# Masks of the scores in a fixed order, the first query load on a second queue, and a planner with other lengths

## The chip, the cores and the metric

The kernel runs on one NeuronCore of a Trainium2 chip. The metric is the device time of one execution in microseconds. The median of three runs of the kernel before is 693.08 us (692.32 to 693.16).

The engines are named as in the profile: PE (matrix multiply; PEld is its weight load), DVE (vector), ACT (scalar), POOL (GpSimd) and SP (the queue that issues nearly all transfers).

## The reference

Windowed attention with four sink keys, over 4 batches, 8 heads, 768 positions and head size 64, is followed by a feed-forward layer over the 3072 tokens (512 to 2048 to 512).

```python
scores = (q @ k.T) / sqrt(64)
keep = (pos_k < n_sink) | ((pos_q - pos_k >= 0) & (pos_q - pos_k < window))   # n_sink 4, window 128
scores = where(keep, scores, -1e9)
a = exp(scores - max); a = a / (sum(a) + 1e-9)
x = (a @ v) with the heads side by side                                     # 3072 x 512
h = x @ w_in                                                                # 512 x 2048
g = where(h >= 1, h, where(h <= -1, 0, (h + 1)**2 / 4))
out = g @ w_out
```

The weights arrive as 64-bit floats and `n_sink` and `window` as 64-bit integers; the kernel takes them apart on the chip.

## The kernel before

**Tiling.** A unit is one batch, one head and 384 query rows, that is three tiles of 128. The first 32 units (query rows 0 to 383 of each head) come first and the other 32 after them. For the first 16 units (batches 0 and 1) two heads make a pair: `pair_scores` (L630 to L673) multiplies queries by keys (L648, PE), adds the mask and takes the row peak (L658, DVE) and does the exponential with its sum (L667, ACT). `pair_sums` (L678, L680, DVE) inverts the sums; `early_transp` transposes the probabilities on PE (L690, L692) and ACT copies them out (L699, L696, L697); `pair_r` and `pair_av` multiply by the inverse sums and the values (L733, L713 on PE, L738 on ACT, L720 on DVE). Four such pairs are one batch, and their result is the tile `xn`. Units of the later batches go through `scores`, `transp` and `av` (L444, L449, L459 to L471, L525, L587).

**Feed-forward.** `split` (L851 ACT, L852 DVE) writes `xn` as a high and a low part `x`, in four pieces of 128 columns. `stage1` (L811 PE) and `stage2` (L834 PE) run over 16 column groups of the hidden layer, each with three matmuls in place of one. Between them stand L818, L819 and L822 on ACT and L820 and L823 on DVE. From the second batch on, this work and the attention of a later batch alternate on PE.

**Weights.** `block(n)` brings one of 16 blocks of 1 MB (L359) and turns it from 64-bit words into a high and a low part: L361, L363, L365 on DVE, L367 on ACT, L368 on DVE. Even blocks belong to `w_in`, odd ones to `w_out`. The first `stage1` needs block 0 and all four pieces of `x` of the first batch, which needs pairs 0 to 3.

**Masks.** Four tiles that hold 0 or a large negative number are made at the start from positions (written by POOL) and from the two parameters `n_f` and `w_f`: `m0` for the first query tile, `m1n` for the second tile of a pair, `m2` for the third, and `m1` for later units.

**What sets the order.** The steps of attention, feed-forward and weights are recorded with `op(engine, length, ...)`. The class `Plan` gives every step a due time, reckoned backwards from PE with the lengths in the code, and writes each engine's queue in the order of a list schedule; a load on SP becomes eligible 3000 or 8000 ns ahead of its due time (L136) and counts as landed 1900 ns after its bytes (L182). After that each engine runs its queue strictly in the order written. The code ahead of the recorded steps (masks, constants) is ordered by the framework. The call that switches that off, `manual_schedule`, stands behind the masks (L398).

Of the kernel before, what the change touches and what calls it, by code (L numbers as in the profile page):

```python
# [197 lines left out]
def attn_ffn(ctx, tc, qk, qkp, vx, vs, par, w_in, w_out, out):  # L198
# [46 lines left out]
    peak = const.tile([P, B * H * NT // CT, CT], F32, name="peak")  # L245

    scr = xpool.tile([P, 1032], F32, name="x")  # L250
    mi = scr[:, 0:260].bitcast(I32)
    rel, kpos, skp, ge0 = scr[:, 260:520], scr[:, 520:648], scr[:, 648:776], scr[:, 776:904]
    ki = scr[:, 904:1032].bitcast(I32)
    nc.gpsimd.iota(mi[:, 0:P], pattern=[[-1, P]], base=P, channel_multiplier=1)
    nc.gpsimd.iota(mi[:, P:KB], pattern=[[-1, NSINK]], base=0, channel_multiplier=0)
    nc.gpsimd.iota(mi[:, KB:260], pattern=[[-1, P]], base=0, channel_multiplier=1)
    nc.vector.tensor_copy(rel, mi)
    nc.gpsimd.iota(ki, pattern=[[1, P]], base=0, channel_multiplier=0)
    nc.vector.tensor_copy(kpos, ki)
    nc.vector.tensor_scalar(skp, kpos, n_f, None, op0=ALU.is_lt)  # L260
    m2 = const.tile([P, 260], F32, name="m2")
    m1 = const.tile([P, 260], F32, name="m1")
    m1n = const.tile([P, 260], F32, name="m1n")
    m0 = const.tile([P, P], F32, name="m0")
# [2 lines left out]
    nc.vector.tensor_tensor(m2[:, KB:260], m2[:, KB:260], ge0, op=ALU.mult)
    nc.vector.tensor_copy(m2[:, P:KB], skp[:, 0:NSINK])
    nc.vector.tensor_copy(m1, m2)
    nc.vector.tensor_copy(m1n, m2)  # L270
    nc.vector.tensor_tensor(m1n[:, 0:P], m2[:, 0:P], skp, op=ALU.max)
    behind = nc.gpsimd.memset(m1n[:, P:KB], 0.0).ins
    nc.vector.tensor_tensor(m0, m2[:, KB:260], skp, op=ALU.max)
    nc.vector.tensor_scalar(skp, kpos, n_f, None, op0=ALU.is_ge)
    nc.vector.tensor_tensor(m1[:, 0:P], m1[:, 0:P], skp, op=ALU.mult)
# [4 lines left out]
    with tc.issue_after(behind):  # L280
        R = 2 * CT * NSINK
        tsel2 = const.tile([120, 2, CT], F32, name="tsel2")
        tsel = const.tile([120, CT], F32, name="tsel")
        nc.gpsimd.memset(tsel2, 0.0)
        for r0 in (0, 32, 64, 96):
            t = tsel2[r0:r0 + R]
            nc.gpsimd.memset(t, 1.0)
            nc.gpsimd.affine_select(out=t, in_=t, pattern=[[-CT * NSINK, 2], [-NSINK, CT]], base=0, channel_multiplier=1,
                                    compare_op=ALU.is_ge, fill=0.0)
            nc.gpsimd.affine_select(out=t, in_=t, pattern=[[CT * NSINK, 2], [NSINK, CT]], base=NSINK - 1,  # L290
                                    channel_multiplier=-1, compare_op=ALU.is_ge, fill=0.0)
        nc.gpsimd.tensor_tensor(tsel, tsel2[:, 0], tsel2[:, 1], op=ALU.add)
        sk1 = const.tile([120, P], F32R, name="sk1")
        nc.gpsimd.memset(sk1.bitcast(F32), 0.0)
        sks = [const.tile([P, 2, CT * NSINK], F32, name=f"sinks{i}") for i in range(2)]
        for t in sks:
            nc.gpsimd.memset(t, 0.0)

        sp = [const.tile([P, CT * P], F32R, name=f"sp{i}") for i in range(2)]
        vsx = [const.tile([P, 2, D], F32R, name=f"vsx{i}") for i in range(2)]  # L300
        for t in sp + vsx:
            nc.gpsimd.memset(t.bitcast(F32), 0.0)
# [775 lines left out]
```

## Time and profile before

| what | value |
|---|---|
| median of three runs | 693.08 us |
| the profiled execution, as timed | 692.49 us |
| its span in the trace | 690.4 us |
| PE busy | 674.4 us, 98% of the span |
| DVE, ACT, POOL busy | 509.6, 487.2, 240.5 us |
| chain that ended last, by engine | PE 90%, DVE 5%, ACT 2%, DMA 1% |

The timed value is 2.1 us above the span and lies inside the spread of the three runs. PE is the engine that is nearly always busy, so the time is read from where PE stands still and from what comes due at those places. A busy share says little about DVE, ACT and the transfers here; their waits in the first 40 us say more. The times in the rows are microseconds from the start of the span.

### The profile page before, as it was taken

How to read it: one execution, taken by the hardware profiler on the slowest of the kernel's cores; microseconds unless marked ns; L12 is line 12 of the kernel's file. 1: busy time of each engine (PE TensorE's matmuls, PEld its weight loads, DVE VectorE, ACT ScalarE, POOL GpSimd, SP SyncE). 2: the span in 40 equal slices, each digit the busy share in tenths (PEclk: the TensorE clock that was granted, in tenths of full speed). 3: DMA queues.
4: the chain of work that ended last, by engine and by line, in shares of the span. 5: the costliest groups of instructions: out<-in, count | busy, mean ns of one | idle time of the engine just before them, and what ended most of it. 6: DMA issues, size and time to landing. Idle time of an engine off the chain costs nothing.

```text
span 690.4 us, 11991 instructions
## 1 busy us (share of the span) xinstructions
PE 674.4 (98%) x3889; PEld 603.1 (87%) x3889; DVE 509.6 (74%) x1421; ACT 487.2 (71%) x1241; POOL 240.5 (35%) x421
## 2 busy tenths in 40 slices
PE   6999999999999999999999999999999999999995
PEld 4677788889999999999999999999999999999994
DVE  7998999887767777787887877887778777733221
ACT  6977776776768788786778777797777866544332
POOL 3000023444434444453553554444463454300000
PEclk9999999999999999999999999999999999999999
DMA  7756353232222433434434443344433231000001
GB/s 230 272 218 217 113 203 105 61 91 62 54 85 91 152 109 103 138 92 142 134 105 121 134 140 94 126 123 134 127 104 104 66 98 33 1 31 16 1 1 51
DMA packets 41086, 73.94 MB, mean 107 GB/s; under 512 B 4344, under 2 KB 25656, under 8 KB 41016
## 3 DMA queue, kind: packets, MB, share of 16 engines
q1 hardware_dynamic: 41016, 73.09, 33.7%
q8 instruction: 33, 0.54, 0.3%
q14 instruction: 37, 0.30, 0.1%
HBM read 66.78 MB, written 6.29 MB: 106 GB/s over the span
## 4 chain that ended last, share of the span: by engine, by line
PE 90%; DVE 5%; ACT 2%; DMA 1%; issue 1%; SPq 0%; POOL 0%; DVEq 0%; ACTq 0%
PE h_ps L811 37%; PE o_ps L834 37%; PE ps_a L587 5%; PE ps_a L444 5%; PE ps_a L525 2%; DMA w<-w_in 1%; PE ps_a L713 1%; PE ps_a L690 1%; PE ps_a L648 1%; DVE x L852 1%; PE ps_a L733 1%; PE ps_a L602 1%; DVE p L471 0%; DMA q_h<-qkp 0%; DVE gl L823 0%
## 5 line engine op out<-in xcount | busy, mean ns | idle before, releaser
L811 PE MATMUL h_ps<-x,wi 128*128 128x384 f32 x1536 | 311.6, 340 | 0.6 <-DVE x L852 0.6
L811 PEld LDWEIGHTS h_ps<-x,wi 128*128 128x128 f32 x1536 | 262.3, 188 | 10.8 <-issue 1.9
L834 PE MATMUL o_ps<-w,gh 128*128 128x512 f32 x768 | 243.4, 398 | 0.0
L834 PE MATMUL o_ps<-w,gl 128*128 128x512 f32 x384 | 151.0, 393 | 0.0
L834 PEld LDWEIGHTS o_ps<-w,gh 128*128 128x128 f32 x768 | 134.1, 188 | 15.7 <-issue 1.4
L426 POOL TENSOR_TENSOR q_l<-r,q_h 128x384 fp32r<-128x384 f32 x48 | 50.1, 1043 | 206.9 <-ACT q_h L425 202.8
L820 DVE SCALAR_TENSOR_TENSOR g<-g,h_ps 128x384 f32<-128x384 f32 x128 | 70.3, 549 | 61.4 <-ACT g L819 60.7
L818 ACT ACTIVATE g<-h_ps,half 128x384 f32<-128x384 f32 x128 | 74.0, 578 | 56.9 <-PE h_ps L811 55.7
L823 DVE TENSOR_TENSOR gl<-g,gh 128x384 fp32r<-128x384 f32 x128 | 78.9, 616 | 31.1 <-ACT gh L822 30.1
L452 ACT ACTIVATE p<-p,peak 128x260 f32<-128x260 f32 (+1 forms) x144 | 71.7, 498 | 40.9 <-DVE peak L449 40.3
L822 ACT CAST gh<-g 128x384 fp32r<-128x384 f32 x128 | 65.3, 510 | 43.8 <-DVE g L820 42.8
L834 PEld LDWEIGHTS o_ps<-w,gl 128*128 128x128 f32 x384 | 72.0, 188 | 16.9
L449 DVE CUSTOM_DVE_ANT_0 p<-ps_a,m 128x260 f32<-128x260 f32 (+1 forms) x144 | 57.6, 408 | 23.6 <-PE ps_a L444 23.2
L819 ACT ACTIVATE g<-g 128x384 f32<-128x384 f32 x128 | 67.3, 526 | 3.5
L471 DVE CUSTOM_DVE_ANT_0 p<-p,stat 128x128 f32<-128x128 f32 x128 | 62.4, 512 | 2.4
L546 POOL TENSOR_SCALAR_AFFINE_SELECT pt<-pt 128x384 fp32r<-128x384 f32 (+1 forms) x96 | 50.8, 535 | 21.8 <-ACT pt L534 12.8
L551 POOL TENSOR_SCALAR_AFFINE_SELECT pt<-pt 128x384 fp32r<-128x384 f32 (+1 forms) x96 | 50.7, 548 | 0.1
L498 POOL TENSOR_TENSOR v_s<-r,v_s 128x256 fp32r<-128x256 f32 (+1 forms) x48 | 37.2, 774 | 37.4 <-ACT v_s L497 31.7
L587 PEld LDWEIGHTS ps_a<-pt,v_s 128*128 128x128 f32 x304 | 42.5, 188 | 2.3
L587 PE MATMUL ps_a<-pt,v_s 128*128 128x256 f32 (+1 forms) x304 | 41.8, 275 | 0.0
L444 PE MATMUL ps_a<-k_s,q_l 128*128 128x260 f32 (+1 forms) x144 | 40.4, 281 | 0.0
L444 PE MATMUL ps_a<-k_s,q_h 128*128 128x260 f32 (+1 forms) x144 | 39.7, 276 | 0.2 <-DVE xn L606 0.2
(158 smaller groups left out, 856.4 us busy)
## 6 DMA issues: line engine op xcount, KB each, us to landing
r<-qk SPq DMA_DIRECT2D x48, 192.0 KB, 2.4
k_r<-qk SPq DMA_DIRECT2D x32, 262.0 KB, 2.8
w<-w_in SPq DMA_DIRECT2D x8, 1024.0 KB, 7.3
again<-w_in SPq DMA_DIRECT2D x16, 512.0 KB, 4.2
again<-w_out SPq DMA_DIRECT2D x16, 512.0 KB, 3.7
w<-w_out SPq DMA_DIRECT2D x6, 1024.0 KB, 7.5
out<-o SPq DMA_DIRECT2D x23, 256.0 KB, 2.9
r<-vx SPq DMA_DIRECT2D x32, 128.0 KB, 2.0
```

Of the source, the lines that this page charges most:

```text
L444: nc.tensor.matmul(ps()[:, lo:260], lhsT=q()[:, i * P:(i + 1) * P], rhs=k_s()[:, c0:c0 + 260 - lo], start=(j == 0), stop=(j == len(qs) - 1))
L449: op(DVE, 215 if lo else 350, lambda: nc.vector.tensor_tensor_reduce(out=p()[:, i, lo:260], in0=ps()[:, lo:260], in1=m, scale=-0.125, scal ...
L452: op(ACT, 400 if lo else 500, lambda: nc.scalar.activation(p()[:, i, lo:260], p()[:, i, lo:260], AF.Exp, bias=peak[:, n, i:i + 1], scale=-1.0,
L471: nc.vector.tensor_tensor_reduce(out=own, in0=own, in1=p()[:, k, 0:P], scale=r, scalar=0.0, op0=ALU.add, op1=ALU.add, accum_out=stat()[:, ...
L587: nc.tensor.matmul(z, lhsT=w, rhs=y, start=(n == 0), stop=(n == len(mms) - 1))
L811: nc.tensor.matmul(h_ps()[:, :T], lhsT=w_i[j][:, w, ct * P:(ct + 1) * P], rhs=x()[:, y, ct], start=(ct == 0 and n == 0), stop=(ct == NCT - ...
L818: op(ACT, 490, lambda: nc.scalar.activation(g(), h_ps()[:, :T], AF.Relu, bias=half, scale=0.5), r=[h_ps], w=[g])
L819: op(ACT, 440, lambda: nc.scalar.activation(g(), g(), AF.Square), w=[g])
L820: op(DVE, 470, lambda: nc.vector.scalar_tensor_tensor(g(), g(), 1.0, h_ps()[:, :T], op0=ALU.min, op1=ALU.max), r=[h_ps], w=[g])
L822: op(ACT, 420, lambda: nc.scalar.copy(gh(), g()), r=[g], w=[gh])
L823: op(DVE, 500, lambda: nc.vector.tensor_tensor(gl(), g(), gh().bitcast(F32), op=ALU.subtract), r=[g, gh], w=[gl])
L834: nc.tensor.matmul(ps(), lhsT=gg()[:, tt * P:(tt + 1) * P], rhs=w_o[j][:, w], start=(j == 0 and n == 0), stop=(j == NJ - 1 and n == 2))
```

## The change

Masks: `manual_schedule` now begins ahead of the masks, so that they stand in the queues as they are written. They are made in fewer steps (for example, `nw` by three small operations in place of five; a comparison and the multiplication by the large negative number in one operation). `m2` and `m1` are finished by three copies on ACT and two operations on POOL. Two clears move from DVE to POOL.

Loads: the parameters and the queries of pair 0 are issued by ACT in place of SP. The query load is not a recorded step: it is written where `pair_load(0)` is called, behind `later_masks()`.

Planner: a weight block whose due time is under 25000 ns becomes eligible 6500 ns ahead in place of 3000 ns, and a block counts as landed 3400 ns after its bytes in place of 1900. The lengths of three kinds of PE steps rise.

```diff
-  max(o.ready, o.due - (3000 if o.due < 25000 else 8000)) if o.eng == SP else o.ready
+  max(o.ready, o.due - (8000 if o.due > 25000 else 6500 if o.bytes == 1 << 20 else 3000)) if o.eng == SP else o.ready
...
-                end = link + 1900
+                end = link + (3400 if o.bytes == 1 << 20 else 1900)
...
+    region.enter_context(tc.manual_schedule())
-    nc.sync.dma_start(par_i, par.rearrange("p (v w) -> p v w", w=2))
+    nc.scalar.dma_start(par_i, par.rearrange("p (v w) -> p v w", w=2))
...
-    nc.vector.tensor_scalar(m2, rel, w_f, None, op0=ALU.is_lt)
...
-    for m in (m0, m1, m1n, m2):
-        nc.vector.tensor_scalar(m, m, -1.0, -NEG, op0=ALU.add, op1=ALU.mult)
+    nc.vector.scalar_tensor_tensor(nw, low, 0.0, high, op0=ALU.is_lt, op1=ALU.add)
+    nc.vector.scalar_tensor_tensor(nw, nw, 2.0 ** 32, low, op0=ALU.mult, op1=ALU.add)
+    nc.vector.tensor_scalar(nw, nw, 0.0, float(S), op0=ALU.max, op1=ALU.min)
+    nc.vector.tensor_scalar(skn, kpos, n_f, NEG, op0=ALU.is_ge, op1=ALU.mult)
+    nc.vector.scalar_tensor_tensor(ahead, rel[:, KB:260], w_f, ahead, op0=ALU.is_ge, op1=ALU.max)
+    nc.vector.tensor_tensor(m0, ahead, skn, op=ALU.mult)
+    nc.vector.scalar_tensor_tensor(m1n[:, 0:P], rel[:, 0:P], w_f, skn, op0=ALU.is_ge, op1=ALU.mult)
+    nc.vector.tensor_scalar(m1n[:, KB:260], ahead, NEG, None, op0=ALU.mult)
+    def later_masks():
+        nc.vector.tensor_scalar(m2[:, 0:P], rel[:, 0:P], w_f, NEG, op0=ALU.is_ge, op1=ALU.mult)
+        nc.scalar.copy(m2[:, P:KB], skn[:, 0:NSINK])
+        nc.scalar.copy(m2[:, KB:260], m1n[:, KB:260])
+        nc.scalar.copy(m1[:, P:260], m2[:, P:260])
+        nc.gpsimd.tensor_scalar(skp, kpos, n_f, NEG, op0=ALU.is_lt, op1=ALU.mult)
+        nc.gpsimd.tensor_tensor(m1[:, 0:P], m2[:, 0:P], skp, op=ALU.add)
+    later_masks()
...
-        op(SP, 420, lambda: nc.sync.dma_start(q_h().bitcast(F32), qkp[b, h // 2, :, 0:T]), w=[q_h], size=P * T * 4)
+        if m:
+            op(SP, 420, lambda: nc.sync.dma_start(q_h().bitcast(F32), qkp[b, h // 2, :, 0:T]), w=[q_h], size=P * T * 4)
+        else:
+            nc.scalar.dma_start(q_h().bitcast(F32), qkp[b, h // 2, :, 0:T])
...
-        op(PE, 340 if lo else 430, mm, r=[q_s, k_s], w=banks)
+        op(PE, (400 if lo else 530) if m < H // 2 else 610 if lo else 840, mm, r=[q_s, k_s], w=banks)
...
-        op(PE, 1400, mm, r=[(pt0[a], "t", k) for a in range(2) for k in range(2)]
+        op(PE, 1450 if m < H // 2 else 1640, mm, r=[(pt0[a], "t", k) for a in range(2) for k in range(2)]
...
-        op(PE, 700, mm, r=[(stat, "r")], w=[ps])
+        op(PE, 750 if m < H // 2 else 1010, mm, r=[(stat, "r")], w=[ps])
...
-        nc.vector.memset(t, 0.0)
+        nc.gpsimd.memset(t, 0.0)
```

The line numbers of the changed kernel are its own: L659 there is L658 before, L679 is L678, L721 is L720, L853 is L852, L457 is L459. L361 to L368 are the same in both. In brackets stands which engine's work an instruction waits for.

**ACT, start of the program.** Before, behind the table load the queue goes straight to the exponentials of pair 0:

```order
L667 ACT_TABLE_LOAD
L667 ACTIVATE p_204,stat_212<-p_204,peak_97 128x128 [waits DVE_49]
L667 ACTIVATE p_210,stat_212<-p_210,peak_97 128x128 [waits DVE_49]
L667 ACTIVATE p_204,stat_212<-p_204,peak_97 128x260 [waits DVE_49] x2
L667 ACTIVATE p_210,stat_212<-p_210,peak_97 128x260
```

and in the changed kernel, from the parameters' load to the first exponential (`x_88` holds `skn`, `q_h_178` the queries of pair 0):

```order
L227 DMA par_i_81<-par 128x4
L272 ACT_TABLE_LOAD
L272 COPY m2_84<-x_88 128x4 [waits DVE_49]
L273 COPY m2_84<-m1n_86 128x128 [waits DVE_49]
L274 COPY m1_85<-m2_84 128x132 [waits Activation_49]
L619 DMA q_h_178<-qkp 128x384
L668 ACTIVATE p_197,stat_205<-p_197,peak_83 128x128 [waits DVE_49]
```

The load of pair 0's queries, which was the third one on SP, stands on ACT behind three copies of masks, two of which wait for DVE.

**DVE, behind the scores of pair 2.** Before (`w_246` is block 0, `stat_285` the sums of pair 1, `xn_163` the output of pair 0):

```order
L361 TENSOR_SCALAR ends_181<-w_246 128x1024
L720 TENSOR_TENSOR xn_163<-ps_a_308,xn_163 128x384
L678 TENSOR_SCALAR stat_285<-stat_285 128x2x3
L680 RECIPROCAL stat_285<-stat_285 128x2x3
L363 TENSOR_SCALAR ends_181<-w_246 128x1024
L365 SCALAR_TENSOR_TENSOR w_246<-w_246,ends_181 128x1024
L658 ISA pt_239,peak_97<-o_ps_355,m0_109 128x128
```

and now (`w_236` is block 0, `stat_275` the sums of pair 1, `ps_a_303` the output of pair 0, `pt_234` and `pt_224` hold pair 3):

```order
L679 TENSOR_SCALAR stat_275<-stat_275 128x2x3
L681 RECIPROCAL stat_275<-stat_275 128x2x3
L721 TENSOR_TENSOR xn_159<-ps_a_303,xn_159 128x384
L361 TENSOR_SCALAR ends_175<-w_236 128x1024
L659 ISA pt_234,peak_83<-o_ps_349,m0_87 128x128
L659 ISA peak_83 128x1
L659 ISA pt_234,peak_83<-o_ps_355,m1n_86 128x260
L659 ISA peak_83 128x1
L363 TENSOR_SCALAR ends_175<-w_236 128x1024
```

The first step of block 0 moved from ahead of the sums and output of pairs 1 and 0 to behind them, and the other two steps moved in among and behind the scores of pair 3.

**DVE, from the sums of pair 2 on.** Before (`stat_328` are these sums, `w_288` is block 1, `w_341` block 2):

```order
L678 TENSOR_SCALAR stat_328<-stat_328 128x2x3
L680 RECIPROCAL stat_328<-stat_328 128x2x3
L363 TENSOR_SCALAR ends_181<-w_288 128x1024
L365 SCALAR_TENSOR_TENSOR w_288<-w_288,ends_181 128x1024
L361 TENSOR_SCALAR ends_181<-w_341 128x1024
L720 TENSOR_TENSOR xn_163<-ps_a_443,xn_163 128x384
L678 TENSOR_SCALAR stat_399<-stat_399 128x2x3
L680 RECIPROCAL stat_399<-stat_399 128x2x3
L368 TENSOR_TENSOR wi0_155<-w_246,wi0_155 128x2x512
L852 TENSOR_TENSOR x_481<-xn_163,x_481 128x384
```

and now (`stat_317` are these sums, `w_236` and `w_277` blocks 0 and 1):

```order
L679 TENSOR_SCALAR stat_317<-stat_317 128x2x3
L681 RECIPROCAL stat_317<-stat_317 128x2x3
L659 ISA pt_234,peak_83<-h_ps_361,m2_84 128x260
L659 ISA peak_83 128x1
L659 ISA pt_224,peak_83<-h_ps_357,m1n_86 128x260
L659 ISA peak_83 128x1
L659 ISA pt_224,peak_83<-o_ps_351,m0_87 128x128
L659 ISA peak_83 128x1
L365 SCALAR_TENSOR_TENSOR w_236<-w_236,ends_175 128x1024
L721 TENSOR_TENSOR xn_159<-ps_a_377,xn_159 128x384
L361 TENSOR_SCALAR ends_175<-w_277 128x1024
```

Three score steps of pair 3, the third step of block 0, the output of pair 1 and the first step of block 1, which stood ahead of these sums, stand behind them now. Up to the fourth `x` piece the last step of block 1 has come in as well; before, it stood behind that piece.

**DVE, first unit of the third batch** (`spare` is the last weight block, `stat` the sums of that unit). Before:

```order
L361 TENSOR_SCALAR ends_181<-spare_182 128x1024
L459 TENSOR_SCALAR stat_1307<-stat_1307 128x3
L462 RECIPROCAL stat_1307<-stat_1307 128x3
L471 ISA p_1299,stat_1307<-p_1299,stat_1307 128x128
L471 ISA stat_1307 128x1
L471 ISA p_1299,stat_1307<-p_1299,stat_1307 128x128
L471 ISA stat_1307 128x1
L469 TENSOR_SCALAR p_1299<-p_1299,stat_1307 128x128
L363 TENSOR_SCALAR ends_181<-spare_182 128x1024
L365 SCALAR_TENSOR_TENSOR ends_181<-spare_182,ends_181 128x1024
```

and now:

```order
L361 TENSOR_SCALAR ends_175<-spare_176 128x1024
L447 ISA p_1298,peak_83<-ps_a_1316,m2_84 128x260
L447 ISA peak_83 128x1
L447 ISA p_1341,peak_83<-ps_a_1320,m0_87 128x128
L447 ISA peak_83 128x1
L363 TENSOR_SCALAR ends_175<-spare_176 128x1024
L365 SCALAR_TENSOR_TENSOR ends_175<-spare_176,ends_175 128x1024
L457 TENSOR_SCALAR stat_1303<-stat_1303 128x3
L460 RECIPROCAL stat_1303<-stat_1303 128x3
L469 ISA p_1298,stat_1303<-p_1298,stat_1303 128x128
L469 ISA stat_1303 128x1
```

The second and third step of the last block moved ahead of the unit's sums. On PE the unit's transposes (L525) moved behind two groups of three L834 matmuls.

## Rows read from the trace of the kernel before

**Rows 1.** Whom PE waited for in the whole span: us in total, times, longest us.
```profile
PE o_ps L648 <- DMA q_h<-qkp: 4.6, 1, 4.6
PE ps_a L690 <- DVE stat L678: 1.6, 1, 1.6
PE ps_a L525 <- DVE p L469: 0.9, 1, 0.9
PE h_ps L811 <- DVE x L852: 0.6, 1, 0.6
```

**Rows 2.** Stretches: length; busy PE, PEld, DVE, ACT, POOL; granted clock; DMA share, GB/s.
```profile
34.00:110.00 76.00, 75.85 (x467) 60.56 (x468) 70.17 (x135) 54.45 (x131) 5.46 (x4) 1.00 0.54 187
150.00:680.00 530.00, 530.00 (x2969) 486.14 (x2968) 375.36 (x1080) 373.99 (x937) 208.58 (x351) 1.00 0.30 90
```

**Rows 3.** The chain that ended last: start, us, what.
```profile
0.79 0.40 SPq L231
...
1.71 2.77 DMA q_h<-qkp
...
8.05 7.46 DMA w<-w_in
...
47.53 1.40 PE o_ps L834 x6
```

**Rows 4.** Whom SP waited for, 0 to 130 us: us in total, times, longest.
```profile
SPq L616 <- PE ps_a L648: 29.5, 5, 15.7
```

**Rows 5.** DVE making masks, in order of time: start, us, instruction, idle before.
```profile
2.53 0.17 DVE L233 CAST par_f<-par_i 128x4 f32<-128x4 int32 x1 [1.35 <-DMA par_i<-par]
...
3.62 0.16 DVE L241 TENSOR_TENSOR nw<-nw,big 128x2 f32<-128x2 f32 x1
3.82 0.29 DVE L260 TENSOR_SCALAR x<-x,nw 128x128 f32<-128x128 f32 x1
...
5.34 0.22 DVE L277 TENSOR_SCALAR m<-m 128x128 f32<-128x128 f32 x1
```

**Rows 6.** PE at the start, in order of time.
```profile
5.61 0.64 PE L648 MATMUL o_ps<-k_s,q_h 64*128 64x260 f32 x1
...
9.17 0.38 PE L648 MATMUL ps_a<-k_s,q_h 64*128 64x260 f32 x1
9.48 0.77 PE L690 MATMUL ps_a<-ident,p 128*128 128x128 f32 x5
```

**Rows 7.** ACT from the first transposes on, in order of time.
```profile
10.06 0.48 ACT L699 COPY pt<-ps_a 128x384 f32<-128x384 f32 x1
...
10.70 0.25 ACT L697 COPY v_s<-ps_a 4x128 f32<-4x128 f32 x1
...
17.54 0.48 ACT L699 COPY pt<-ps_a 128x384 f32<-128x384 f32 x1 [0.99 <-PE ps_a L690]
...
20.31 0.51 ACT L667 ACTIVATE p<-p,peak 128x260 f32<-128x260 f32 x1
```

**Rows 8.** DVE around the first blocks and `x` pieces, in order of time.
```profile
15.61 0.76 DVE L361 TENSOR_SCALAR ends<-w 128x1024 uint8<-128x1024 uint8 x1 [2.08 <-DMA w<-w_in]
16.24 0.54 DVE L720 TENSOR_TENSOR xn<-ps_a,xn 128x384 f32<-128x384 f32 x1
...
21.87 0.16 DVE L678 TENSOR_SCALAR stat<-stat 128x6 f32<-128x6 f32 x1
...
33.34 0.53 DVE L852 TENSOR_TENSOR x<-xn,x 128x384 fp32r<-128x384 f32 x1
```

**Rows 9.** DVE by line, 21.8 to 34 us: busy, mean ns, idle before and its releaser.
```profile
L365 DVE SCALAR_TENSOR_TENSOR w<-w,ends 128x1024 int32<-128x1024 int32 x2 | 2.5, 1236 | 0.1
L368 DVE TENSOR_TENSOR wi<-w,wi 128x1024 fp32r<-128x1024 f32 x2 | 2.4, 1222 | 0.4 <-ACT wi L367 0.4
...
L720 DVE TENSOR_TENSOR xn<-ps_a,xn 128x384 f32<-128x384 f32 x3 | 1.6, 547 | 0.5 <-PE ps_a L713 0.5
L363 DVE TENSOR_SCALAR ends<-w 128x1024 uint8<-128x1024 uint8 x2 | 1.5, 743 | 0.0
...
L658 DVE CUSTOM_DVE_ANT_0 p<-ps_a,m1n 128x260 f32<-128x260 f32 x1 | 0.4, 408 | 0.0
```

More of the change, by code (lines that the diff above doesn't have):

```diff
@@ L135, in open_ @@
             if o.eng != PE:
-                heapq.heappush(later[o.eng], (max(o.ready, o.due - (3000 if o.due < 25000 else 8000)) if o.eng == SP else o.ready, o.n, o))
+                heapq.heappush(later[o.eng], (max(o.ready, o.due - (8000 if o.due > 25000 else 6500 if o.bytes == 1 << 20 else 3000)) if o.eng == SP else o.ready, o.n, o))
         def head(x):
@@ L227, in attn_ffn @@
     nc.gpsimd.memset(half, 0.5)
-    par_i = const.tile([P, 2, 2], I32, name="par_i")
-    nc.sync.dma_start(par_i, par.rearrange("p (v w) -> p v w", w=2))
+    nc.vector.tensor_copy(rel, mi)
+    nc.vector.tensor_copy(kpos, ki)
+    nc.vector.tensor_scalar(ahead, rel[:, KB:260], 0.0, None, op0=ALU.is_lt)
     par_f = const.tile([P, 2, 2], F32, name="par_f")
@@ L245, in attn_ffn @@
[L245 to L264, printed above, removed]
-    nc.vector.tensor_scalar(m2, rel, w_f, None, op0=ALU.is_lt)
-    nc.vector.tensor_scalar(ge0, rel[:, KB:260], 0.0, None, op0=ALU.is_ge)
@@ L267, in attn_ffn @@
[L267 to L275, printed above, removed]
@@ L276, in attn_ffn @@
-    for m in (m0, m1, m1n, m2):
-        nc.vector.tensor_scalar(m, m, -1.0, -NEG, op0=ALU.add, op1=ALU.mult)
[L280 to L302, printed above, removed]
@@ new lines, in attn_ffn @@
+    later_masks()
+    R = 2 * CT * NSINK
+    tsel2 = const.tile([120, 2, CT], F32, name="tsel2")
+    tsel = const.tile([120, CT], F32, name="tsel")
+    nc.gpsimd.memset(tsel2, 0.0)
+    for r0 in (0, 32, 64, 96):
+        t = tsel2[r0:r0 + R]
+        nc.gpsimd.memset(t, 1.0)
+        nc.gpsimd.affine_select(out=t, in_=t, pattern=[[-CT * NSINK, 2], [-NSINK, CT]], base=0, channel_multiplier=1,
+                                compare_op=ALU.is_ge, fill=0.0)
+        nc.gpsimd.affine_select(out=t, in_=t, pattern=[[CT * NSINK, 2], [NSINK, CT]], base=NSINK - 1,
+                                channel_multiplier=-1, compare_op=ALU.is_ge, fill=0.0)
@@ new lines, in attn_ffn @@
+    nc.gpsimd.tensor_tensor(tsel, tsel2[:, 0], tsel2[:, 1], op=ALU.add)
+    sk1 = const.tile([120, P], F32R, name="sk1")
+    nc.gpsimd.memset(sk1.bitcast(F32), 0.0)
+    sks = [const.tile([P, 2, CT * NSINK], F32, name=f"sinks{i}") for i in range(2)]
+    for t in sks:
+        nc.gpsimd.memset(t, 0.0)
+    sp = [const.tile([P, CT * P], F32R, name=f"sp{i}") for i in range(2)]
+    vsx = [const.tile([P, 2, D], F32R, name=f"vsx{i}") for i in range(2)]
+    for t in sp + vsx:
+        nc.gpsimd.memset(t.bitcast(F32), 0.0)
@@ L890, in attn_ffn @@
     for t in spn:
-        nc.vector.memset(t, 0.0)
+        nc.gpsimd.memset(t, 0.0)
     ends = dec.tile([P, 2, DM], I32, name="ends")
     spare = dec.tile([P, 2, 2 * DM], I32, name="spare")
-    with tc.issue_after(behind):
-        nc.gpsimd.memset(ends, 0)
+    nc.gpsimd.memset(ends, 0)
     p0 = [p_ring.new() for _ in range(2)]
```

25 lines of the change are left out of this document (17 added, 8 removed).

## The prediction

> **What bounds the kernel now.** I read first whom PE waited for, since PE is busy for 98% of the span (the table above). The list is short [rows 1]: 4.6 us at the start for the queries of pair 0, 1.6 us near 16 us behind the sums of a pair, 0.6 us near 33 us for a piece of `x`, and 0.9 us near 114 us. Then I read the stretches [rows 2]: from 34 to 110 us PE is busy for 75.85 of 76 us, and from 150 to 680 us all the time. So the kernel is a full PE queue behind an opening of 34 us, and the changed kernel has the same matmuls in nearly the same order. The difference is what the opening gains or loses, plus the 0.9 us.
>
> What sets the opening is read from the chain [rows 3] and from three queues. PE starts when `q_h` has landed, 2.77 us after its issue at 1.71. Block 0 is asked for at 8.05 and takes 7.46 us, and DVE, which has it next in its queue, stands still for 2.08 us [rows 8]. From there to the fourth piece of `x` at 33.34 DVE has hardly a gap, and PE's wait of 0.6 us ends on that piece [rows 1, 8]. So behind the first block DVE sets when PE can run freely.
>
> **The load of pair 0's queries** is the largest term. On ACT it stands behind three copies, the second of which needs the last step of `m1n`. The parameters reach DVE at 2.53 [rows 5]; they came by the same small load and I leave that time as it is. Then follow the cast (0.17) and three small steps that each wait for the one ahead, 0.20 apart as L241 and L260 are [rows 5], so `n_f` and `w_f` stand at about 3.3. Five mask steps up to the end of `m1n` follow, of 0.22 to 0.29 us each with neighbours partly overlapped [rows 5]: 4.4 to 4.7. No copy of 128 columns on ACT is in the trace; 4 columns take 0.25 and 384 take 0.48 [rows 7], so the two copies that are left take 0.5 to 0.7 and the load is issued near 5.0 (4.8 to 5.4). The landing of a load that ACT issues is not in the trace either; from SP it took 2.77 [rows 3], with two loads ahead of it and two more right behind. Alone it may take some tenths less, and I take 2.6, with 2.3 and 2.9 as ends. PE starts at 7.7 (7.2 to 8.3) in place of 4.62: **+3.1 us**.
>
> That a load is held by the wait of what stands ahead of it is plain on SP: a key load waited five times for PE, up to 15.7 us [rows 4], with all later loads behind it. The Trainium skill says in "DMA: Bandwidth & Descriptors", section "Issuing engines are not separate DMA queues", that issuing from several engines only saves the sequencer time of the issue; by that rule alone the second queue gives about 0.9 us, as the second rival has it, and costs nothing.
>
> **What the masks give back.** Before, the scores waited for masks: `m0` was done at 5.56 [rows 5], though PE had started at 4.62, and mask steps stood between the scores. In the changed kernel all masks that pairs 0 and 1 need are ready before PE starts, so this wait goes; the two copies, two POOL operations and the moved clears lie in time when nobody needs them. From PE's first matmul to the first transposes it was 4.86 us (9.48 less 4.62) [rows 1, 6], and I take 4.55 now. It can't fall much, since PE itself is slow there: the same 260 columns take 0.64 us at 5.61 and 0.38 at 9.17 [rows 6]. PE had stood idle until 4.62; I let as many matmuls be slow as before. The transposes begin at 12.25: **+2.8 us**. If the slow matmuls ended at the old clock time instead, the two pairs would take some 1.5 us less. The Trainium skill has a rule on this ("TensorE: Matmul & The Clock Gate", Part 1): the slow level of 1.2 GHz is the default and activity releases it; that favours the later end.
>
> **Where the stall near 16 us goes.** The first step of block 0 now stands behind the sums of pair 1 and the output of pair 0, so PE's 1.6 us wait for them is gone, also if block 0 lands late. It will: its load stands on SP behind the keys of pair 2, which wait for pair 0's scores, and behind one load more than before; with 7.46 us of flight it lands near 19 instead of 15.5. PE reaches the scores of pair 3 only +1.2 us late. But ACT and DVE do not get that back. ACT runs from the first transposes (10.06) to the last exponential of pair 2 (20.31, done by 20.9 with its sum) with one gap of 0.99, ended by PE's stall [rows 7]. Shifted by 2.75, without the gap, and with one 0.4 us copy moved behind, it ends at 20.9 + 2.75 - 0.99 - 0.4 = 22.25. That is when DVE can run the sums of pair 2, at 21.87 before [rows 8].
>
> **Behind those sums DVE has more to do than before.** From their start to the end of the fourth `x` piece it was 12.0 us (21.87 to 33.87) [rows 8], of which 0.9 were waits for ACT and PE [rows 9], so 11.1 of work. In the changed queue the same stretch also holds one L365 (1.24), one L368 (1.22), one output step (0.55), one L361 (0.76) and three score steps (at most 0.41 each): 5.0 by the means [rows 8, 9]. Neighbours overlap, as L361 and L720 do by 0.13 [rows 8], so I take 4.4. Work that was done in DVE's stall and idle ahead of the sums is now behind them. 22.3 + 11.1 + 4.4 = 37.8 in place of 33.87: **+3.9**. The two ends of the start (7.2, 8.3) and of the extra work (4.0, 5.0) make it +3.0 to +5.1.
>
> **From there on** PE's queue is as full as before. One step of block 1 that stood behind the fourth `x` piece is already done, 1.2 us to the good for DVE. At the first unit of the third batch, L363 and L365 (0.74 + 1.24) now stand ahead of the sums, and PE has six L834 matmuls (1.40) [rows 3] more to do before it needs them. So the wait of 0.93 there becomes about 0.93 - 1.2 + 2.0 - 1.4 = 0.3: **-0.6**, between -0.9 (gone) and +0.8. The earlier requests of weight blocks I cost at nothing: DVE's only wait for a block was that for block 0, and what hides the others is DVE's own backlog; without that cover an early request would save its wait, of which the trace has none. The planner's lengths do nothing by themselves.
>
> Sum: +3.9 - 0.6 = +3.3 on the profiled execution's 692.5 gives 695.8; the median of before lies 0.6 above that execution. I predict **696.0**, +2.9 on the median, the low side of the sum, since DVE's queue may have waits filled that I count as work.
>
> **The rivals.**
> *The delay is absorbed* (not slower). Decided by DVE: if the sums of pair 2 come by 20 us, or the steps behind them have shorter waits than I think, PE's own shift at the scores of pair 3 stands, 2.8 less 1.6, so +1.2, and -0.6 later: +0.6, 693.7. For it speaks that PE's wait of 1.6 near 16 us goes; against it that DVE was without a gap from 15.6 to 33.9 already [rows 8]. A shorter slow stretch on PE would lead here too.
> *The load isn't held* (faster). If the issue on ACT passes the waiting copies, the queries land up to 0.9 us sooner, since the parameters' load at 0.79 and one key load no longer stand ahead on SP (issue at 1.71) [rows 3]. PE starts near 3.8, the masks are the limit at 4.2 to 4.6, and the chain over block 0 and DVE moves by 0.4; with the 0.6 later it is -1.0: 692.1. The built queue and [rows 4] speak against it.
> *The later queue is worse.* Two block steps (1.5 us) now stand at several places ahead of the steps between the two layers. If PE ends up waiting for one of these, and the wait at 114 us grows by the 0.8, another 2 us come: 698.0. Against it, PE waited for none of them before [rows 1].
>
> **How the numbers follow.** Forecast 0.63 (694.8 to 697.3), absorbed 0.17, not held 0.07, worse 0.13. A measurement of this kernel can tell about 0.2%, 1.4 us, from no change, so "slower" is above 694.5. The worse case and nearly all of the forecast are slower: 0.74. The absorbed case is the same, with a part of the forecast's low end and of the second rival: 0.19. Faster is 0.07. The range holds the forecast, the absorbed case's upper half and the lower half of the worse case: 693.4 to 698.0.
>
> **What would show it.** Right: PE's first wait is 7.2 to 8.3 us and ends on `q_h`; the load is issued by ACT near 5.0; PE's wait for the sums near 16 us is gone; the fourth `x` piece ends near 37.5 on DVE; from 40 to 110 us PE has no gap. Wrong: PE starts by 4.6, which would mean the second rival; or it starts at 7.7 and the fourth `x` piece still ends by 35.5, which would mean that DVE has slack that I did not see.

## The result and the profile after

The changed kernel takes 696.92 us (median of 4 runs, 696.70 to 698.34); the kernel before took 692.80 beside it. The ratio is 1.0066, with a 95% interval of 1.0049 to 1.0082, so the change costs 3.4 to 5.7 us. In a second comparison the ratio was 1.0053 (1.0039 to 1.0066). The profiled execution took 696.81 us with a span of 695.0, 4.6 more than before. The forecast was 696.0, with 693.4 to 698.0 as its range.

Whom PE waited for, in the changed kernel (us in total, times, longest), answers [rows 1]:

```profile
PE o_ps L649 <- DMA q_h<-qkp: 8.5, 2, 8.1
PE ps_a L691 <- DVE xn L721: 2.3, 3, 1.0
PE ps_a L523 <- DVE p L467: 1.1, 1, 1.1
PE h_ps L812 <- DVE x L853: 0.6, 1, 0.6
PE ps_a L691 <- ACT pt L668: 0.4, 1, 0.4
```

The wait for pair 0's queries went from 4.6 to 8.1 us. The wait of 1.6 for the sums near 16 us is gone. The wait at 114 us (now L523, near 120 us) is still there, a little longer. New are a second wait for queries (8.5 less 8.1) and three for `xn`.

Stretches of the changed kernel (length; busy PE, PEld, DVE, ACT, POOL; granted clock; DMA share, GB/s), beside [rows 2]:

```profile
0.00:34.00 34.00, 22.98 (x205) 17.15 (x207) 23.23 (x85) 24.86 (x86) 7.41 (x38) 1.00 0.71 238
34.00:110.00 76.00, 75.00 (x468) 58.44 (x463) 72.56 (x139) 54.78 (x133) 5.25 (x4) 1.00 0.54 186
110.00:125.00 15.00, 13.94 (x77) 12.50 (x76) 11.11 (x29) 9.37 (x26) 5.08 (x7) 1.00 0.24 78
125.00:150.00 25.00, 25.00 (x145) 23.04 (x144) 21.02 (x68) 20.95 (x58) 12.02 (x23) 1.00 0.22 62
150.00:680.00 530.00, 529.62 (x2966) 485.37 (x2965) 369.33 (x1086) 376.23 (x938) 208.36 (x355) 1.00 0.30 91
```

Length less busy PE is PE's idle time. The trace of before gives 7.27, 0.15, 0.93, 0.34 and 0.00 us for the five stretches, and this one 11.02, 1.00, 1.06, 0.00 and 0.38. The differences are +3.75, +0.85, +0.13, -0.34 and +0.38: 4.77 us, of which 4.60 lie ahead of 110 us. The rest of the 4.6 of the span is a busy time that is 0.1 longer and a tail that is 0.27 shorter.

The head of the chain that ended last (start, us, what) takes the place of the first lines of [rows 3]:

```profile
0.79 2.29 DMA par_i<-par
...
3.10 0.18 DVE par_f L255
...
5.07 0.23 DVE m1n L268
5.30 0.02 issue
5.33 0.31 ACT m L273
5.63 0.02 issue
5.66 0.01 ACT m L274
5.66 2.32 DMA q_h<-qkp
7.98 0.14 issue
8.12 1.19 PE o_ps L649 x5
```

Before, the chain began with the issue of the load. Now the whole making of the masks stands ahead of it: parameters, nine steps on DVE, a copy on ACT and the start of the next, and only then the load of the queries.

Further on in the changed kernel (PE, ACT and DVE, in order of time), beside [rows 6 to 8]:

```profile
12.18 0.64 PE L649 MATMUL ps_a<-k_s,q_h 64*128 64x260 f32 x1
12.75 0.78 PE L691 MATMUL ps_a<-ident,p 128*128 128x128 f32 x5
...
14.69 0.38 PE L649 MATMUL h_ps<-k_s,q_h 64*128 64x260 f32 x1
...
20.42 0.68 PE L649 MATMUL o_ps<-k_s,q_h 64*128 64x128 f32 x5 [0.42 <-DMA q_h<-qkp]
...
37.98 1.14 PE L812 MATMUL h_ps<-x,wi 128*128 128x384 f32 x5 [0.62 <-DVE x L853]
```

```profile
19.35 0.75 DVE L361 TENSOR_SCALAR ends<-w 128x1024 uint8<-128x1024 uint8 x1 [0.32 <-DMA w<-w_in]
...
22.69 0.17 DVE L679 TENSOR_SCALAR stat<-stat 128x6 f32<-128x6 f32 x1
...
37.38 0.55 DVE L853 TENSOR_TENSOR x<-xn,x 128x384 fp32r<-128x384 f32 x1
```

PE's matmuls of 260 columns take 0.64 until 12.18 and 0.38 by 14.69. The transposes begin 4.63 us after PE's start, the sums of pair 2 are at 22.69, and the fourth `x` piece ends at 37.93 in place of 33.87. PE stands for it as before, 0.62 us, so the delay of the opening passes whole.

### The profile page after: what moved, and what is told of

Its sections match the earlier page's. It is cut to its first block, busy times and chain, and to the rows that moved or that the text cites. A ratio compares the mean times of both kernels' runs of the same rounds, so it can differ in the third digit from the quotient of the medians.

```text
span 695.0 us, 11990 instructions
## 1 busy us (share of the span) xinstructions
PE 674.6 (97%) x3889; PEld 603.0 (87%) x3889; DVE 499.4 (72%) x1409; ACT 489.6 (70%) x1244; POOL 238.1 (34%) x425
## 4 chain that ended last, share of the span: by engine, by line
PE 85%; DVE 7%; DMA 3%; ACT 2%; issue 1%; POOL 0%; SPq 0%; ACTq 0%
PE h_ps L812 35%; PE o_ps L835 35%; PE ps_a L585 5%; PE ps_a L442 4%; PE ps_a L523 2%; DMA q_h<-qkp 1%; DMA r<-qk 1%; DVE ends L363 1%; DVE w L365 1%; DVE wi L368 1%; PE ps_a L714 1%; PE o_ps L649 1%; PE ps_a L649 1%; DVE ends L361 1%; DVE p L469 1%
## 5 line engine op out<-in xcount | busy, mean ns | idle before, releaser
L835 PEld LDWEIGHTS o_ps<-w,gh 128*128 128x128 f32 x768 | 134.0, 188 | 15.5 <-issue 1.4
L469 DVE CUSTOM_DVE_ANT_0 p<-p,stat 128x128 f32<-128x128 f32 x128 | 57.3, 475 | 2.2
L544 POOL TENSOR_SCALAR_AFFINE_SELECT pt<-pt 128x384 fp32r<-128x384 f32 (+1 forms) x96 | 48.9, 512 | 23.2 <-ACT pt L532 11.8
L496 POOL TENSOR_TENSOR v_s<-r,v_s 128x256 fp32r<-128x256 f32 (+1 forms) x48 | 34.9, 728 | 48.1 <-ACT v_s L495 45.9
L549 POOL TENSOR_SCALAR_AFFINE_SELECT pt<-pt 128x384 fp32r<-128x384 f32 (+1 forms) x96 | 50.2, 543 | 0.1
```

What stands on the lines that cost most here:

```text
L469: nc.vector.tensor_tensor_reduce(out=own, in0=own, in1=p()[:, k, 0:P], scale=r, scalar=0.0, op0=ALU.add, op1=ALU.add, accum_out=stat()[:, ...
L835: nc.tensor.matmul(ps(), lhsT=gg()[:, tt * P:(tt + 1) * P], rhs=w_o[j][:, w], start=(j == 0 and n == 0), stop=(j == NJ - 1 and n == 2))
```

## The experiments

My theory: the load of pair 0's queries is held behind the mask copies, and that is nearly all of the loss. Rivals: the new order of the queues costs by itself; PE's first, slow stretch takes back what an earlier start gives. Each kernel below the first row was timed in five rounds beside the kernel before, which had medians from 692.66 to 692.98 in these comparisons.

| kernel | median us | ratio to before (95%) | PE starts at |
|---|---|---|---|
| changed kernel | 696.92 | 1.0066 (1.0049 to 1.0082) | 8.12 |
| the same once more | 696.77 | 1.0053 (1.0039 to 1.0066) | 8.15 |
| copies behind the load | 692.86 | 1.0003 (0.9994 to 1.0012) | 4.72 |
| query load back on SP | 692.40 | 0.9990 (0.9979 to 1.0001) | 4.12 |
| before, load held | 695.35 | 1.0038 (1.0026 to 1.0050) | 8.08 |
| before, planner's numbers | 692.03 | 0.9985 (0.9974 to 0.9997) | 4.81 |
| changed, old planner's numbers | 695.89 | 1.0051 (1.0037 to 1.0064) | 8.16 |
| parameters on SP, queries on ACT | 692.39 | 0.9989 (0.9980 to 0.9999) | 4.29 |
| copies behind, unit 18 off POOL | 693.57 | 1.0004 (0.9993 to 1.0014) | 4.95 |
| the last two together | 692.21 | 0.9986 (0.9977 to 0.9995) | 3.99 |
| both loads as before | 691.39 | 0.9976 (0.9965 to 0.9988) | 4.84 |
| loads as before, unit 18 off POOL | 690.84 | 0.9969 (0.9959 to 0.9979) | 4.84 |
| masks alone | 691.77 | 0.9986 (0.9974 to 0.9997) | 4.7 |

### Is it the place of the load?

Copies behind the load: three instructions on ACT move, and every queue keeps its order otherwise.

```diff
     def later_masks():
...
-        nc.scalar.copy(m2[:, P:KB], skn[:, 0:NSINK])
-        nc.scalar.copy(m2[:, KB:260], m1n[:, KB:260])
-        nc.scalar.copy(m1[:, P:260], m2[:, P:260])
...
+    def mask_copies():
+        nc.scalar.copy(m2[:, P:KB], skn[:, 0:NSINK])
+        nc.scalar.copy(m2[:, KB:260], m1n[:, KB:260])
+        nc.scalar.copy(m1[:, P:260], m2[:, P:260])
...
     run([("A", 1.0, first_pairs)], 0)
+    mask_copies()
```

> The changed kernel with one thing different: the load of pair 0's queries stands ahead of the three mask copies in ACT's queue. Every other instruction stands in the changed kernel's place. Theory (the hold): the load is issued near 1.3 instead of 5.66, lands by 3.6 to 3.9, PE starts near 3.9, the first score step waits for the mask m0 until about 4.9, and the fourth piece of x on DVE ends between 32.8 and 34.2 (37.93 in the changed kernel, 33.87 before). Time 691.8 to 693.4. Rival (the new order of the queues costs by itself, since DVE has block steps ahead of the pair sums): the piece ends at 35.5 or later whatever PE's start is, time 694.5 or more. Rival (PE's slow first stretch): pairs 0 and 1 take as much longer as PE starts sooner, the transposes start at 10.5 or later instead of about 9, time 693.5 to 694.5.

Measured: 692.86, at the level of before, 4.06 us below the changed kernel. So the hold is the loss, and the new order does not cost it. PE's slow first stretch takes nothing back either: the transposes began at 9.35, not at 10.5 or later. Two details missed. The fourth `x` piece ends at 34.78, later than I had it, and the load did not come sooner than before:

```profile
0.79 0.40 ACTq L227
1.18 0.03 issue
1.21 3.38 DMA q_h<-qkp
4.59 0.14 issue
4.72 1.19 PE o_ps L651 x5
```

Issued half a microsecond sooner than in [rows 3], it flew 3.38 us in place of 2.77. One key load stood ahead of it here (0.79) as in the kernel before (1.24), but a second one was issued beside it, at 1.24; before, the second came 0.47 later than the queries.

Query load back on SP: one line of `pair_load` undone, the parameters still on ACT. The load is a planned step again, so the orders of DVE, ACT, POOL and SP shift in places as well.

```diff
-        if m:
-            op(SP, 420, lambda: nc.sync.dma_start(q_h().bitcast(F32), qkp[b, h // 2, :, 0:T]), w=[q_h], size=P * T * 4)
-        else:
-            nc.scalar.dma_start(q_h().bitcast(F32), qkp[b, h // 2, :, 0:T])
+        op(SP, 420, lambda: nc.sync.dma_start(q_h().bitcast(F32), qkp[b, h // 2, :, 0:T]), w=[q_h], size=P * T * 4)
```

> The changed kernel with the load of pair 0's queries back in SP's planned queue, behind one key load; the parameters stay on ACT. Theory (the hold is the whole loss): PE starts between 4.2 and 4.8 and the time is 692.0 to 693.2. Rival (the later parameters, 3.10 in place of 2.53, and the new order keep a part of the loss): the first score step on DVE is at 5.6 or later and the time 693.8 or more.

Measured: 692.40. PE starts at 4.12, sooner than expected, since the load is issued at 1.24 behind one key load and flies 2.75. The first score step on DVE is at 5.47, not 5.6 or later. The loss is gone again.

Before with the load held, of the whole change the hold alone. The load is no planned step here, so the orders of DVE, ACT, POOL and SP shift in places:

```diff
-        op(SP, 420, lambda: nc.sync.dma_start(q_h().bitcast(F32), qkp[b, h // 2, :, 0:T]), w=[q_h], size=P * T * 4)
+        if m:
+            op(SP, 420, lambda: nc.sync.dma_start(q_h().bitcast(F32), qkp[b, h // 2, :, 0:T]), w=[q_h], size=P * T * 4)
+        else:
+            nc.scalar.copy(hold, m0[:, 0:4])
+            nc.scalar.dma_start(q_h().bitcast(F32), qkp[b, h // 2, :, 0:T])
```

> The kernel before, masks and all, with one part of the change alone: the load of pair 0's queries is issued by ACT, behind a copy of four columns of the finished mask m0. So the load leaves near 5.9 and PE starts near 8.3 (4.62 before). Theory (the hold): that is the whole cost, 695.5 to 697.2. Rival (absorbed): without the new order DVE's stall of 2.1 us for the first block and PE's wait of 1.6 us near 16 us swallow part of it, 693.6 to 695.

Measured: 695.35, +2.7 on before. The hold makes most of the loss without any other part of the change: PE starts at 8.08 and the fourth `x` piece ends at 37.79, both as in the changed kernel. That is just below the range of my theory and above that of the rival.

### What does the planner's order cost?

The numbers alone in the kernel before, and the old numbers in the changed kernel (the other way round). The three PE lengths go with them:

```diff
-  o.due - (3000 if o.due < 25000 else 8000)
+  o.due - (8000 if o.due > 25000 else 6500 if o.bytes == 1 << 20 else 3000)
-  end = link + 1900
+  end = link + (3400 if o.bytes == 1 << 20 else 1900)
```

> The kernel before with the planner's numbers of the change alone (when a weight block may be asked for, how long it is taken to need, and PE's step lengths). Loads and masks are those of before. Theory (the hold): the order alone does next to nothing, 692.3 to 693.6, and a wait of 0.3 to 1.1 us stays near 110 us. Rival (the new order costs by itself): 694.5 or more, with the fourth piece of x at 35 or later.

> The changed kernel with the planner's numbers of the kernel before: new masks and loads, with the query load behind the copies, and the old rules for the order. Theory (the hold): PE starts at 8.1 as in the changed kernel and the time is within 0.7 of it, 696.2 to 697.6. Rival (the new order costs by itself): 693.5 to 695.3.

Measured: 692.03 and 695.89. The first is below the range of my theory, the second between those of theory and rival. The order is no loss in the kernel before; by its interval it is a small gain of 0.2 to 1.8 us. With the held load, the old order's ratio is 1.0051 and the new one's 1.0066 and 1.0053, and these intervals overlap. In the trace with the old order the fourth `x` piece ends at 36.41 in place of 37.93, from the same start of PE. So whether the new order costs something beside a held load, up to about 1 us, stays open.

### What is left of the change without the two loads?

Both loads as before: the query load back on SP as above, and the parameters ahead of it. In the second kernel the old planner's numbers as well:

```diff
-    nc.scalar.dma_start(par_i, par.rearrange("p (v w) -> p v w", w=2))
+    nc.sync.dma_start(par_i, par.rearrange("p (v w) -> p v w", w=2))
```

> The changed kernel with both loads where they were before: parameters first on SP, then the keys and the queries of pair 0. What is left of the change is the masks by fewer steps and the planner's numbers. Theory (the loads do all the harm, and a small load is early only if no big one flies beside it): the parameters reach DVE at 2.5, m0 is done by 4.3, PE starts at 4.5 to 4.8, and the first score step on DVE is at 5.0 to 5.3, sooner than before (its m0 was done at 5.56). Time 691.2 to 692.3, less than the 692.7 of before. Rival (nothing of the masks reaches the end, since ACT and DVE set the opening further on): within 0.3 of the kernel before with the planner's numbers alone, 692.0.

> The run with the loads as before, with the planner's numbers of the kernel before as well: of the whole change only the masks by fewer steps are left. Theory (masks and order each give a part): the masks take four steps off DVE between the score steps of pair 0 (6.15 to 7.0 us before), so the last exponential of pair 0 ends near 9.2 in place of 9.9, and the time is 691.6 to 692.4, between the kernel before and the run with the loads as before (691.4). Rival (the order gives it all): 692.5 or more.

Measured: 691.39 and 691.77, both faster than before. In the trace of the first of them, ACT's exponentials of pair 0 (in order of time):

```profile
5.98 0.40 ACT L665 ACTIVATE p<-p,peak 128x128 f32<-128x128 f32 x1 [0.47 <-DVE peak L656]
...
8.58 0.50 ACT L665 ACTIVATE p<-p,peak 128x260 f32<-128x260 f32 x1
8.98 0.19 ACT L665 ACTIVATION_READ_ACCUMULATOR p<-p,peak 128x1 f32 x1
```

They end at 9.17; before they ended at 9.92, with 0.49 and 0.30 of idle, in which DVE made masks between the score steps. Masks and order both differ here: with the masks alone they end at 9.37, with 0.22 and 0.26 of idle. The first score step is not sooner (5.64; PE sets it), which my expectation had wrong.

How the masks' gain reaches the end is not shown. In the trace of the masks alone the transposes begin at 9.36 (9.48 before). Then block 0, issued at 8.11 in place of 8.05, landed at 14.76 in place of 15.51, and DVE's steps behind it keep that lead up to the fourth `x` piece (33.11 in place of 33.87). No row ties the shorter flight to the masks, and it is one execution of each kernel.

So the masks alone (-1.0 by the medians, 0.2 to 1.8 by the interval) and the order alone (-0.6, the same interval) are small gains. That they add up is not shown: 691.39 is 0.4 below the masks alone, and the intervals overlap. Moving the two loads turned the gain into a loss of 4.1. Of the two, the hold is most of it; the run with the query load back on SP has the queues of 691.39 but for the parameters' load and is 1.0 above it, with intervals that overlap.

### Does an earlier issue bring an earlier landing?

Parameters on SP, queries first on ACT. On top of the copies behind the load:

```diff
-    nc.scalar.dma_start(par_i, par.rearrange("p (v w) -> p v w", w=2))
+    nc.sync.dma_start(par_i, par.rearrange("p (v w) -> p v w", w=2))
```

> The changed kernel with the copies behind the query load (as in the run with the copies behind), and the parameters issued by SP ahead of everything, as in the kernel before. So ACT issues the queries at 0.79, 0.42 earlier than in that run, and SP the first keys at 1.24. Theory A (the first loads share the wire, so that issuing sooner only lets them fly longer): the queries land at 4.3 or later, the flight is 3.4 us or more, and PE starts no sooner than 4.3; the parameters reach DVE at 2.5 to 2.6, the masks are done by 4.7, and the time is 692.2 to 693.0. Theory B (the landing goes by the issue, 2.8 us after it): PE starts at 3.6 to 4.0 and the time falls to 691.2 to 692.0.

Neither theory held as written. The queries, issued at 0.79, flew 2.6 us, as B has it; PE then waited for the keys (1.24, 2.91 us) and started at 4.29. The parameters were issued at 0.79 as in [rows 3] and yet came a microsecond later than in [rows 5]. First the row of this kernel, then that of both loads as before:

```profile
3.57 0.17 DVE L255 CAST par_f<-par_i 128x4 f32<-128x4 int32 x1 [1.54 <-DMA par_i<-par]
```

```profile
2.66 0.17 DVE L255 CAST par_f<-par_i 128x4 f32<-128x4 int32 x1 [0.63 <-DMA par_i<-par]
```

In these runs the load of 2 KB was early where it was issued 0.45 us or more ahead of every large one, and late where a large one was issued at the same moment on the other queue.

### PE's wait near 115 us

Here the prediction had 0.3 us and the changed kernel 1.06. DVE and POOL of the changed kernel, in order of time:

```profile
116.13 1.63 DVE L363 TENSOR_SCALAR ends<-spare 128x1024 uint8<-128x1024 uint8 x1
117.80 1.90 DVE L365 SCALAR_TENSOR_TENSOR ends<-spare,ends 128x1024 int32<-128x1024 int32 x1
119.62 0.15 DVE L457 TENSOR_SCALAR stat<-stat 128x3 f32<-128x3 f32 x1
```

```profile
116.12 1.03 POOL L424 TENSOR_TENSOR q_l<-r,q_h 128x384 fp32r<-128x384 f32 x1 [14.05 <-ACT q_h L423]
117.22 1.40 POOL L421 TENSOR_TENSOR k_s<-k_r,k_s 64x392 fp32r<-64x392 f32 x1
```

The two block steps take 3.53 us together where [rows 9] have 0.74 and 1.24, and each overlaps a POOL subtraction. The test puts these two subtractions on DVE, behind the sums:

```diff
-        pool = units.index(u) in KL_POOL
+        own = units.index(u) == 18
+        pool = units.index(u) in KL_POOL and not own
...
-        op(POOL, 1020, lambda: nc.gpsimd.tensor_tensor(q_l(), q_r(), q_h().bitcast(F32), op=ALU.subtract), r=[q_r, q_h],
+        op(DVE if own else POOL, 800 if own else 1020, lambda: (nc.vector if own else nc.gpsimd).tensor_tensor(
+            q_l(), q_r(), q_h().bitcast(F32), op=ALU.subtract), r=[q_r, q_h],
```

> The run with the copies behind, with one more thing different: the two subtractions of unit 18 (keys and queries), which ran on POOL from 113.0 to 115.5 us, are on DVE, where they stand behind the pair's sums. DVE's queue up to those sums is the same. Theory (DVE stands still while POOL runs): the two block steps ahead of the sums take 0.75 and 1.23 again, in place of 1.62 and 1.90, PE's wait there falls from 1.06 to 0 to 0.3, and the time falls by 0.6 to 1.1, to 691.6 to 692.3. Rival (the steps are slow by their operands, or the chain of PE, DVE and ACT sets the wait whatever POOL does): the steps stay above 1.5 and 1.8, or they get short and the wait stays above 0.8; time 692.5 to 693.3.

> Both of these together: parameters on SP, queries first on ACT, copies behind, and unit 18's subtractions on DVE. Theory (the two gains are in different places and add): the time is that of the run with the parameters on SP less 0.6 to 1.1, 691.2 to 692.2, below the kernel before. Rival (what the opening gains is given back later): within 0.3 of the run with the copies behind.

> The run with the loads as before, with unit 18's two subtractions on DVE as well. In the runs with that edit PE's wait near 115 us went from 1.06 to nothing, and yet the time fell little. Theory (what PE gains there it loses again in pieces of 0.1 to 0.3 us in the next 200 us, where the other engines are not ahead): 0 to 0.4 less than the run without this edit, with its PE 1.0 to 1.3 ahead near 118 us and at most 0.5 ahead near 600. Rival (the gain stands, the earlier pair of runs was disturbed): 0.8 to 1.2 less.

DVE in the first of the three:

```profile
112.72 0.77 DVE L365 TENSOR_SCALAR ends<-spare 128x1024 uint8<-128x1024 uint8 x1
113.53 1.23 DVE L367 SCALAR_TENSOR_TENSOR ends<-spare,ends 128x1024 int32<-128x1024 int32 x1
114.67 0.16 DVE L461 TENSOR_SCALAR stat<-stat 128x3 f32<-128x3 f32 x1
```

The steps are short again, and PE's wait is gone in all three. So POOL's work stretches DVE's; the rival on the operands falls. The Trainium skill states this in "SBUF — State Buffer", section "Who interferes with whom": certain DVE operations and GpSimd share ports that whoever starts first holds for a whole instruction. The trace agrees in the main: 1.63 is POOL's 1.03 plus 0.60, a little under the 0.77 that the step takes alone.

The trace of the kernel before has the same overlap at the same place, which I had overlooked. DVE, then POOL:

```profile
111.46 1.43 DVE L361 TENSOR_SCALAR ends<-spare 128x1024 uint8<-128x1024 uint8 x1
112.78 0.99 DVE L459 TENSOR_SCALAR stat<-stat 128x3 f32<-128x3 f32 x1
```

```profile
111.23 1.03 POOL L426 TENSOR_TENSOR q_l<-r,q_h 128x384 fp32r<-128x384 f32 x1 [8.87 <-ACT q_h L425]
112.34 1.41 POOL L423 TENSOR_TENSOR k_s<-k_r,k_s 64x392 fp32r<-64x392 f32 x1
```

Elsewhere these two DVE steps take 0.76 and 0.16, so POOL accounts for some 1.5 us ahead of PE's wait of 0.93 there too. That is read from the rows; the kernel before was not run without the overlap.

The time did not follow as expected. The medians are 693.57 against 692.86 without the edit, 692.21 against 692.39, and 690.84 against 691.39; no pair of intervals is apart, and the 0.55 of the last lies between theory and rival. In the last pair, where PE's order is the same, PE reaches its next twelve L811 matmuls (L809 in the one without the edit) at 116.27 in place of 117.94, 1.67 ahead, of which 0.35 was there at 52 us already. At 174 us it is 0.44 ahead, and at 598 us still 0.44. Most of it was lost here (PE, in order of time); the lead is 1.69 at the first of these two rows and 0.85 behind the second:

```profile
139.13 0.22 PE L444 MATMUL ps_a<-k_s,q_h 128*128 128x128 f32 x1
139.97 0.33 PE L444 MATMUL ps_a<-k_s,q_l 128*128 128x128 f32 x1 [0.62 <-POOL q_l L425]
```

POOL's subtraction for a later unit comes at 138.90 in place of 135.07. Its queries go through `r`, of which there is one buffer; unit 18 gives it back at about 118 now, not 113. That this is why it came late is argued from the order and was not tried alone. The rest of the lead went in steps that the waits do not name; the orders of the other engines shift with this edit too.

The changed kernel once more:

> The changed kernel once more, beside the two others on one chip: 696.2 to 697.4. Theory (the loads): the run with the loads as before is 4.2 to 5.5 below it. Its PE should start between 8.0 and 8.2 again, and the time from PE's start to the end of the slow matmuls should vary by up to 2 us between executions of one program, as it did between programs.

Measured: 696.77, 5.4 us above the run with both loads as before. PE started at 8.15. Its matmuls of 260 columns were at 0.38 from 11.68 on; in the first profile of the same program the last of 0.64 began at 12.18:

```profile
11.30 0.52 PE L649 MATMUL o_ps<-k_s,q_h 64*128 64x260 f32 x1
...
11.68 0.38 PE L649 MATMUL ps_a<-k_s,q_h 64*128 64x260 f32 x1
12.21 0.77 PE L691 MATMUL ps_a<-ident,p 128*128 128x128 f32 x5
```

Both spans are 695.0. So the 0.54 us by which the transposes came sooner did not reach the end: PE's second wait for queries was 1.4 in place of 0.42, and DVE's wait for block 0 was 1.27 in place of 0.32. Behind a late start, loads and DVE set the opening.

## Why the prediction was right, and where it was not

**The direction and the size** were right, by the mechanism that was named: the load is held behind the copies in ACT's queue, and the opening passes the delay on. The first run shows it: with three copies moved, the loss is gone. Of the signs that the prediction named, one failed: PE has a gap between 40 and 110 us, 0.37 at 100.15, behind an exponential on ACT.

**PE's start** was 8.12, forecast 7.7 (7.2 to 8.3). The issue at 5.66 lies outside its range of 4.8 to 5.4. The step that failed is "I leave that time as it is": the parameters reached DVE at 3.10, not 2.53. Without these 0.57 the issue is at 5.09, inside. The copies were sized from a misread row: `4x128` in [rows 7] is 128 columns on 4 partitions, not 4 columns. The last two copies ahead of the load (128 and 132 columns on 128 partitions) took 0.30 each, and the load left as the second of them began, 0.37 behind the end of `m1n`, where the prediction has 0.5 to 0.7. The landing took 2.32, the low end, and hid part of the late parameters too.

**The transposes** began 4.63 after PE's start, forecast 4.55. PE's slow start was kept, as assumed. What the masks give back was judged right. Where all matmuls of 260 columns up to the transposes take 0.64, the time is 4.62 to 4.68 with the new masks or the held load (copies behind 4.63, masks alone 4.68, before held 4.62) and 4.93 with neither (before, planner's numbers). With both loads as before it is 3.78, but there these matmuls are at 0.38 from 7.85 on; the earlier end of the slow stretch shortens it, and not the masks.

**ACT and DVE**: the exponentials of pair 2 were done at 22.49 (forecast 22.25) and the sums were at 22.69 (22.3). From there to the end of the fourth `x` piece it took 15.24 (15.5): DVE was busy for 14.90, 4.0 more than in the same stretch before (forecast 4.4, 4.0 to 5.0), and idle for 0.34. So the extra work that DVE does behind those sums was sized right. The piece ended at 37.93 (37.8): +4.06 for +3.9. That PE's start came 0.42 late and the piece only 0.13 is luck in part: later terms erred the other way.

**The wait near 114 us** was the term that was mis-sized: -0.6 forecast (-0.9 to +0.8), +0.13 measured. I gave the two block steps 0.74 and 1.24, their means; beside POOL they took 1.63 and 1.90, and with the short steps the wait was gone in three runs. The wait of 0.93 that the sum starts from stood beside the same POOL steps, so it did not come of DVE's backlog alone. The 1.2 us that DVE was to have in hand brought nothing either: by then DVE had run out of work, and ahead of these steps it stood for 2.61 and 1.21 us for PE's scores.

**Earlier requests of weight blocks cost nothing** failed in two ways. Pair 3's query load stood behind block 0 and took 7.05 us, and PE waited 0.42 for it at 20.42, which I did not foresee. In the kernel before it stood behind block 0 too (6.59), but PE came later by its stall near 16 us. With the old planner's numbers and the held load it was issued ahead of block 0, took 2.74, and PE did not wait. In the kernel before, the same numbers bring a small gain (0.6 by the medians).

On the profiled executions the sum, 695.8, is 1.0 below the result, 696.81: 0.73 from the wait near 114 us, 0.16 from the `x` piece, and the rest in waits too short for any step of the sum (the 0.38 behind 150 us are two of 0.2).

**The rivals**: "the delay is absorbed" needed the sums of pair 2 by 20 us; they were at 22.69. "The later queue is worse" had the wait near 114 us grow by 0.8; it grew by 0.13. "The load isn't held" gave 692.1 for the case that the queries are not late; the runs with a free load are at 692.4 and 692.9. Its reason was wrong where both loads are on ACT: the second queue brought no earlier landing there. In the run at 692.4 PE did start 0.5 sooner, since the parameters no longer stood ahead of the queries on SP. That is what the rule on issuing engines cited in the prediction says ("DMA: Bandwidth & Descriptors" in the Trainium skill, "Issuing engines are not separate DMA queues"). The trace with the copies behind the load agrees that a second queue gives no more than that: 0.5 sooner at the issue, 0.1 later at PE.

## What to carry to other kernels

Before a load goes to another engine's queue, read what that engine has ahead of it: here the load behind three copies left when the inputs of the last copy were there, 5.66 us in place of 1.71. Measure the parts of a change one by one; here two small gains (1.0 and 0.6 us by the medians, each alone) were hidden by the move of two loads, which cost five. Where a DVE step is costed by its mean, look whether POOL works beside it.

## What the runs showed of the hardware

- A load of 2 KB took 1.64 to 1.85 us as the first on SP, 2.28 to 2.37 from ACT with key loads beside it on SP, and 2.76 from SP with a query load beside it on ACT. A load of 192 KB took 2.32 alone, 3.38 with one key load ahead of it and one right behind, and 7.05 behind a block of 1 MB.
- A DVE step that overlaps a POOL subtraction was stretched from 0.77 to 1.63 and from 1.23 to 1.90 us; in the kernel before, one of 128x3 from 0.16 to 0.99.
- After PE's idle start, matmuls of 260 columns took 0.64 at first and 0.38 later. The granted clock is printed as 1.00 in both stretches, so no row shows that the first ones ran at the lower of the clock's two levels (1.2 and 2.4 GHz). In one execution of the changed kernel the last of 0.64 began at 12.18; in another they were at 0.38 from 11.68 on. What decides this was not tried.
